# Unread products in TensorE's planned gaps, five early weight tiles, and the block mask as rows of the second score product

## Chip, core and metric

The kernel runs on one core of one Trainium2 chip. The metric is the device time of one execution in microseconds (us). The kernel before was timed at 738.15 us, the median of three runs from 735.75 to 738.77 us.

## What is computed

Three blocks follow one another on 4 sequences of 576 tokens. All inputs are float32.

```python
# attention: 8 heads of 64, causal by blocks of 64 tokens
scores = where(q_block >= k_block, q @ k.T / 8, -1e9)
x = softmax(scores) @ v                      # heads side by side: 512 features
# first mixture block, x_prev is x one token earlier
xk = mu_k * x + (1 - mu_k) * x_prev
xr = mu_r * x + (1 - mu_r) * x_prev
x = sigmoid(xr @ w_r) * (relu(xk @ w_k) ** 2 @ w_v)
# second mixture block
h = gelu_tanh(x @ w_in); u, v = halves(h)
out = x + (u * (w_sg @ layernorm(v) + b_sg)) @ w_out
```

## The kernel before

**Precision.** A float32 product is made of single-pass products in float32r: each operand is split into a high part and the rest, and three products are summed (high by high, high by rest, rest by high). The weights come as float64 words; `w_split` turns one tile of 128 x 512 of them into such a pair with two passes on ScalarE, four on VectorE and one on GpSimd. There are 20 such tiles for the first mixture block: 8 of `w_k`, 4 of `w_r`, 8 of `w_v`.

**Attention units.** A unit is one head of one sequence with either its first 320 tokens (`LO`, block rows 0 to 2) or its last 256 (`HI`, block rows 3 and 4); there are 64. The first 16 (`n < DIRECT`) are the `LO` units of sequences 0 and 1: their scores are plain float32 products, and two extra rows of the operands (66 rows in all) carry the block mask. For the other 48 units q and k lie twice, on partitions 0 to 63 and 64 to 127. `split_qk` makes `Q` (high part above, rest below), `K` (high part in both halves) and `KL` (the rest of k in both halves); `emit_S` then adds `Q` by `K` and `Q` by `KL` in PSUM, and between the two, for each block row but the first, a third product of 64 columns from `mask_l` and `mask_r`, which puts -2**33 on the last 64 columns for the first 64 queries of the row. That is two mask products a unit, 96 in all. Then come the maximum (VectorE), the exponential (ScalarE), the norm (VectorE), the transposes (`emit_T`) and the product with v (`emit_PV`), which writes the PSUM tile `O`; ScalarE copies `O` out to `xT`.

**Order.** Python code first lists all operations in an order of preference (`Order`, `attention`, `moe1`). `Plan.schedule` then simulates the engines with fixed costs (`takes`, `cost`) and lists every operation at its planned time, taking on each engine the ready operation that stands first in the list. That order is emitted; each engine works through its part of it strictly in order, and waits on the chip where the plan was too early. All loads go through SyncE's queue (SP). A weight load is planned behind the load that was listed before it (`op.behind`). The operations of all lines are emitted by one statement, so in the profile they all stand under L460, and the tile names tell them apart.

**First phase.** The eight `LO` heads of sequence 0 run first while the weights arrive; the heads' raw tiles share the ring `qkv` of three buffers (the first four heads use borrowed tiles). Then `moe1` works through eight halves of 288 tokens, with the attention units of the other sequences interleaved. Each half has the products with `w_k`, then `w_r`, then `w_v`. PSUM pool `ps1` serves all this and is closed at the start of the second mixture block.

The loads before the first attention step are issued by

```python
for n in range(5):
    load_head(n)
take(loads, 1)
```

and after that each second piece of attention work takes one more weight load.

Of the kernel before, what the change touches and what calls it, by code (L numbers as in the profile page):

```python
# [27 lines left out]

SHARE = dict(Kh=0.5, Qs=0.25, psc=0.25, xls=0.25)
calls = {}


# [39 lines left out]

class View:
# [195 lines left out]
    return d - 45, d, fn != "memset"  # L275


class Engine:
    def __init__(self, plan, name):
        self.plan, self.name = plan, name  # L280
# [5 lines left out]
class Plan:  # L286
# [2 lines left out]


    def __init__(self, tc):
        self.tc, self.nc, self.ops, self.last_dma = tc, tc.nc, [], None
        for e in ENG:
            setattr(self, e, Engine(self, e))

# [30 lines left out]
    def gate(self, closes, opens):  # L326
# [2 lines left out]
        self.ops.append(op)  # L329
        return op  # L330

    def schedule(self):
        for op in self.ops:
            if op.alts[0][0] == "gate":
                for p in op.alts[0][1]:
                    for o in p.ops:
                        op.preds[o.n] = o
        for op in self.ops:
            op.preds.pop(op.n, None)
            op.left = len(op.preds)  # L340
            for p in op.preds.values():
                p.succs.append(op)
        soon = {e: [] for e in ("PE", "ACT", "DVE", "POOL", "SP", "NONE")}
        ripe = {e: [] for e in soon}
        free = {e: 0.0 for e in soon}
        lock = dict(DVE=0.0, POOL=0.0)
        dma = 0.0
        order = []

        def offer(op):  # L350
            for x in op.tiles:
                if x.since is None:
                    x.waiters.append(op)
                    if len(x.waiters) == 1:
                        pump(x.ring)
                    return
            for i, a in enumerate(op.alts):
                e = ENG.get(a[0], "NONE")
                t = op.ready
                if op.preds:  # L360
                    t = max((p.run[0] if e == p.bi == "PE" or p is op.behind else p.end + LAT[e]) for p in op.preds.values())
                t = max([t] + [x.since + LAT[e] for x in op.tiles])
                heapq.heappush(soon[e], (t, op.n, i))

        def pump(ring):
            for x in ring.grant():
                for op in x.waiters:
                    offer(op)

        for r in {x.ring for op in self.ops for x in op.tiles}:  # L370
            r.tiles = [x for x in r.tiles if x.ops]
            for x in r.tiles:
                x.todo = len(x.ops)
        for op in self.ops:
            if not op.left:
                offer(op)
        while True:
            best = None
            for e in soon:
                for h in (ripe[e], soon[e]):  # L380
                    while h and self.ops[h[0][1] if h is soon[e] else h[0][0]].done:
                        heapq.heappop(h)
                if ripe[e]:
                    t = free[e]
                elif soon[e]:
                    t = max(free[e], soon[e][0][0])
                else:
                    continue
                if best is None or t < best[0]:
                    best = t, e  # L390
            if best is None:
                break
            t, e = best
            while soon[e] and soon[e][0][0] <= t:
                _, n, i = heapq.heappop(soon[e])
                heapq.heappush(ripe[e], (n, i))
            while self.ops[ripe[e][0][0]].done:
                heapq.heappop(ripe[e])
                if not ripe[e]:
                    break  # L400
            if not ripe[e]:
                continue
            n, i = heapq.heappop(ripe[e])
            op = self.ops[n]
            op.done, op.bi = True, e
            order.append((op, i))
            if e == "NONE":
                op.run, op.end = (t, t), t
            elif op.alts[i][1] == "dma_start":
                a = op.alts[i][2]  # L410
                v = next(x for x in a.values() if isinstance(x, View))
                rows = v.shape[0]
                size = v.cols * rows * 4 if not v.tile.dram else v.cols * 4
                if e == "SP":
                    free[e] = t + 375
                dma = max(t + 1400, dma) + size / (250.0 if rows != 66 else 172.0)
                op.run, op.end = (t, t + 375), dma + 150
            else:
                busy, d, port = takes(e, *op.alts[i][1:])
                s = t  # L420
                if port:
                    o = "POOL" if e == "DVE" else "DVE"
                    s = max(t, lock[o])
                end = max(s + d, t + d)
                free[e] = max(s + busy, end - (d - busy))
                if port:
                    lock[e] = end - (150 if e == "DVE" else 0)
                op.run, op.end = (s, free[e]), end
            for x in op.tiles:
                x.end = max(x.end, op.end)  # L430
                x.todo -= 1
                if not x.todo:
                    x.ring.slots.append(x.end)
                    pump(x.ring)
            for q in op.succs:
                q.left -= 1
                if not q.left:
                    offer(q)
        if len(order) < len(self.ops):
            o = next(o for o in self.ops if not o.done)  # L440
            seen = []
            while o not in seen:
                seen.append(o)
                o = next((p for p in o.preds.values() if not p.done), None) or next(
                    p for x in o.tiles if x.since is None for y in x.ring.tiles for p in y.ops if not p.done and p is not o)
            raise ValueError([(o.n, o.alts[0][:2], [(k, x.tile.args["tag"]) for k, x in o.alts[0][2].items() if isinstance(x, View)]) for o in seen[seen.index(o):]])
        self.order = order
        return max(o.end for o in self.ops)
# [49 lines left out]
def cost(n):  # L498
    return n / 2.4 + 13
# [3 lines left out]
def fused_kernel(ctx: ExitStack, tc: tile.TileContext, first, qkv_lo, qkv_hi, mu,  # L503
# [18 lines left out]
    def ptile(tag, cols, bufs):  # L522

        r = ring.setdefault(tag, [])
        if len(r) >= bufs:
            order.need(("ps", tag, len(r) - bufs))
        key = ("ps", tag, len(r))
        r.append(key)
        return ps([128, cols], F32, tag, bufs), key


    att_over = []
# [31 lines left out]
    nc.gpsimd.affine_select(out=ident, in_=ident, pattern=[[-1, 128]], compare_op=ALU.is_equal,  # L564
                            fill=0.0, base=0, channel_multiplier=1)

    mask_l = const([128, 128], F32R, "mask_l")
    mask_r = const([128, 64], F32R, "mask_r")
    nc.gpsimd.memset(mask_l.bitcast(F32), 0.0)
    nc.gpsimd.memset(mask_l[0:1, 0:64].bitcast(F32), 1.0)  # L570
    nc.gpsimd.memset(mask_r.bitcast(F32), -2.0 ** 33)
    mu_t = const([128, 2, 4], F32, "mu_t")
    um_t = const([128, 2, 4], F32, "um_t")
    x2d = [dram([4, 128, S], F32, f"x2d{b}") for b in range(B)]

    pcm, ps = pool("ps1", space=PSUM)
    mcm, mtile = pool("moe1")
    acm, atile = pool("attn", side="right")

# [11 lines left out]
    for t in pbuf:  # L591
        nc.gpsimd.memset(t[64:128, 0:64], 0.0)


    w1 = {}

# [62 lines left out]
    def split_qk(n):  # L659
# [4 lines left out]
        nq, nk = q.shape[1], k.shape[1]  # L664
        Q = atile([128, 320], F32R, "Q", 2)[:, 0:nq]
        K = atile([128, S], F32R, "K", 2)[:, 0:nk]
        KL = atile([128, S], F32R, "KL", 2)[:, 0:nk]
        copy(nc.scalar, Q, q)
        copy(act("Kh") if units[n][2] == HI else nc.scalar, K, k)
        sub(dve("Qs"), Q[64:128, :], q[64:128, :], Q[64:128, :].bitcast(F32))  # L670
        sub(nc.gpsimd, KL, k, K.bitcast(F32))
        splits[n] = (Q, K, KL)

    def split_v(n):
# [10 lines left out]

    def score_ns(n):
        f, cs = (2, CHUNKS[units[n][2]]) if n >= DIRECT else (4, CHUNKS[LO])
        return sum(f * cost(e - a) for c in cs for a, e in PIECES[c]) + cost(64) * (f == 2) * sum(c > 0 for c in cs)

    def out_ns(n, trans=True):  # L690
        kind = units[n][2]
# [3 lines left out]
    def emit_S(n):  # L695
# [18 lines left out]
        for c in chunks:  # L714
            q0, m, e, st = CH0[c] - TOKENS[kind][0], CHN[c], CHE[c], stc[c]
            for k0, k1 in PIECES[c]:
# [2 lines left out]
                    mm(o, Q[:, q0:q0 + m], K[:, k0:k1], start=True, stop=True)  # L719
                    continue  # L720
                mm(o, Q[:, q0:q0 + m], K[:, k0:k1], start=True)
                if c > 0 and k1 == e:
                    mm(st[:, e - 64:e], mask_l, mask_r)
                mm(o, Q[:, q0:q0 + m], KL[:, k0:k1], stop=True)

        def red(cs):
            for c in cs:
# [178 lines left out]
    def moe1():  # L906
# [3 lines left out]
        for i, (b, f) in enumerate(halves):  # L910
# [3 lines left out]
            for m in range(8):  # L914
# [18 lines left out]
                    nc.scalar.activation(out=R, in_=p, func=AF.Relu)  # L933

                def e1(R=R):
                    nc.scalar.activation(out=R, in_=R, func=AF.Square)

                def e2(R=R, m=m, kh=kh, kl=kl):
                    copy(nc.scalar, kh[:, m, :], R)
# [21 lines left out]
            for m in range(4):  # L961
# [3 lines left out]
                for g in range(0, 8, G):  # L965
# [2 lines left out]
                    pe(3 * G * cost(HF))  # L968
                    spent += 3 * G * cost(HF)
                    passes(p, "wv", 8, m, kh, kl, g, g + G)  # L970
                x2 = mtile([128, HF], F32, "x2", 2)

                def e4(p=p, m=m, x2=x2, th=th, b=b, f=f):
                    nc.vector.scalar_tensor_tensor(out=x2, in0=th[:, m, :], scalar=1.0, in1=p,
# [39 lines left out]
    early = [t[:, i] for tag in ("kh", "kl") for t in [mtile([128, 2, 960], F32, tag, 1)] for i in range(2)]  # L1014
    for n in range(5):
        load_head(n)
    take(loads, 1)
    nc.vector.tensor_scalar(out=um_t, in0=mu_t, scalar1=-1.0, scalar2=1.0, op0=ALU.mult, op1=ALU.add)
    split_qk(0)
    k = 0  # L1020
# [73 lines left out]
                pair(0, t, f * HF, (f + 1) * HF)  # L1094
    take(conv2, 99)
    order.run()
    pcm, ps = pool("ps2", space=PSUM, after=[pcm])
    ring.clear()

# [264 lines left out]
```

## Time and profile before

| | |
|---|---|
| median of 3 runs | 738.15 us |
| profiled execution | 739.07 us |
| its span, first to last instruction | 737.3 us |
| mean granted TensorE clock | 0.972 |
| busy share: matmul, weight load, VectorE, ScalarE, GpSimd | 95, 89, 72, 61, 41% |

PE is TensorE's matmul stream and PEld its weight loads; DVE is VectorE, ACT is ScalarE, POOL is GpSimd, SP is SyncE's queue. The shares are means over the whole span; the first 140 us differ from the rest. A granted clock of 1.00 is 2.4 GHz and 0.50 is 1.2 GHz. The 1.00 that the views give for the first stretch is a default and not a reading: two records of the product SB<-kh of 66 x 320 take 1.27 us at 5.01 us, and those of SB<-qkv of the same shape 0.70 us at 19.33 us. A float32 product stands in the trace as two matmul records, and some records are missing.

### The profile page before, as it was taken

The numbers are of one execution on the slowest core, as the hardware profiler recorded it, in microseconds if no ns is written. First come the engines' busy times: TensorE is split into PE (matmuls) and PEld (weight loads), VectorE is DVE, ScalarE is ACT, GpSimd is POOL, SyncE is SP. The second block draws the span as 40 slices with busy tenths as digits, with TensorE's granted clock in tenths as the row PEclk, the third lists the DMA queues.
The fourth block names the chain that finished last, engine by engine and source line by source line (L and its number), as shares of the span: only waits on it lengthen the run. The fifth ranks groups of instructions, "written<-read, shape, count | busy, mean of one in ns | idle before, by whom it ended". The sixth has DMA issues, their size and how long they took to land. (4 is left out here: it accounts for less than half of the span.)

```text
span 737.3 us, 13563 instructions
## 1 busy us (share of the span) xinstructions
PE 696.8 (95%) x4824; PEld 656.8 (89%) x4824; DVE 534.2 (72%) x1306; ACT 451.8 (61%) x1279; POOL 300.3 (41%) x349
## 2 busy tenths in 40 slices
PE   7859877899999999999999999999999999999998
PEld 5648665899999999999999999998898998998998
DVE  4888868788888777787888789679699546546323
ACT  3868755799689689799799689666353022022020
POOL 1235436576466346456567447132025012013021
PEclk9978886999999999999999999999999999999999
DMA  6196111522222222223231321072640120210101
GB/s 171 53 332 210 36 33 33 186 73 97 82 91 70 85 64 71 87 86 96 90 107 65 113 81 33 12 243 72 235 165 1 64 66 1 67 63 1 65 1 65
DMA packets 30722, 65.77 MB, mean 89 GB/s; under 512 B 5280, under 2 KB 16544, under 8 KB 30656
## 3 DMA queue, kind: packets, MB, share of 16 engines
q1 hardware_dynamic: 30512, 64.91, 27.4%
q8 instruction: 38, 0.62, 0.4%
q14 instruction: 28, 0.23, 0.1%
q10 hardware_dynamic: 144, 0.00, 0.0%
HBM read 55.47 MB, written 9.44 MB: 88 GB/s over the span
## 5 line engine op out<-in xcount | busy, mean ns | idle before, releaser
L460 PE MATMUL M<-xh,w 128*128 128x288 f32 x704 | 173.7, 313 | 5.9 <-ACT xh L460 2.5
L460 PEld LDWEIGHTS M<-xh,w 128*128 128x128 f32 x704 | 123.9, 194 | 9.0 <-ACT xh L460 2.8
L460 PE MATMUL M<-kh,w 128*128 128x288 f32 x432 | 106.3, 313 | 2.5 <-ACT w L460 1.3
L460 PE MATMUL M<-xl,w 128*128 128x288 f32 x352 | 107.1, 305 | 0.0
L460 PE MATMUL T<-ident,P 128*128 128x128 f32 x480 | 80.6, 286 | 12.8 <-DVE P L460 9.0
L460 DVE TENSOR_SCALAR_CACHE_REDUCE P<-P,rr 64x64 f32<-64x64 f32 (+3 forms) x160 | 79.6, 537 | 1.5
L460 POOL TENSOR_TENSOR KL<-qkv,K 128x576 fp32r<-128x576 f32 (+1 forms) x48 | 61.5, 1282 | 44.3 <-ACT K L460 35.3
L460 PEld LDWEIGHTS M<-kh,w 128*128 128x128 f32 x432 | 75.1, 192 | 4.5 <-ACT w L460 1.9
L460 ACT ACTIVATE PH<-T 128x384 fp32r<-128x384 f32 (+4 forms) x144 | 67.3, 478 | 19.1 <-PE T L460 17.9
L460 PEld LDWEIGHTS T<-ident,P 128*128 128x128 f32 x480 | 59.5, 145 | 20.9 <-DVE PL L460 8.7
L460 DVE TENSOR_TENSOR PL<-T,PH 128x256 fp32r<-128x256 f32 (+3 forms) x128 | 67.5, 543 | 13.6 <-ACT PH L460 12.6
L460 POOL TENSOR_TENSOR kl<-R,kh 128x288 fp32r<-128x288 f32 x64 | 56.1, 878 | 41.5 <-ACT kh L460 36.5
L460 PEld LDWEIGHTS M<-xl,w 128*128 128x128 f32 x352 | 68.7, 195 | 0.5 <-DVE u L460 0.2
L460 POOL TENSOR_TENSOR gt<-gt,U 128x288 f32<-128x288 f32 x32 | 28.2, 884 | 99.7 <-DVE gt L460 97.6
L460 POOL TENSOR_TENSOR w<-u,w 128x512 fp32r<-128x512 f32 x24 | 36.4, 1516 | 75.7 <-ACT w L460 65.9
L460 PE MATMUL M<-kl,w 128*128 128x288 f32 x216 | 65.4, 303 | 0.0
L460 POOL TENSOR_TENSOR xl<-t,xh 128x288 fp32r<-128x288 f32 x48 | 40.5, 843 | 58.9 <-ACT xh L460 53.8
L460 ACT ACTIVATE U<-M 128x288 f32<-128x288 f32 x32 | 13.0, 410 | 71.7 <-PE M L460 71.7
L460 PE MATMUL O<-gh,w 128*128 128x288 f32 x256 | 52.4, 297 | 1.0 <-DVE o L460 1.0
L460 DVE SCALAR_TENSOR_TENSOR u<-w,u 128x512 int32<-128x512 int32 x64 | 51.9, 817 | 0.2
L460 PE MATMUL M<-XHL,w 128*128 128x288 f32 x384 | 51.9, 295 | 0.0
L460 PE MATMUL O<-PH,V 128*128 128x256 f32 (+2 forms) x208 | 51.5, 278 | 0.1
(182 smaller groups left out, 1935.1 us busy)
## 6 DMA issues: line engine op xcount, KB each, us to landing
qkv<-qkv_hi_dram SPq DMA_DIRECT2D x32, 576.0 KB, 3.6
qkv<-qkv_lo_dram SPq DMA_DIRECT2D x16, 416.0 KB, 3.4
x2d<-x SPq DMA_DIRECT2D x32, 144.0 KB, 1.8
X<-x2d SPq DMA_DIRECT2D x4, 1152.0 KB, 12.3
outT_dram<-o SPq DMA_DIRECT2D x32, 144.0 KB, 1.8
w<-w_k_dram SPq DMA_DIRECT2D x8, 512.0 KB, 11.1
w<-w_v_dram SPq DMA_DIRECT2D x8, 512.0 KB, 9.5
w<-w_in_dram SPq DMA_DIRECT2D x8, 512.0 KB, 8.6
```

The lines of the kernel that those rows point to most:

```text
L460: getattr(getattr(self.nc, e), fn)(*pos, **{k: real(x) for k, x in a.items() if k[0] != "_"})
```

## The change

The fillers: `plan.fill` names one product, 64 x 192 from a tile `calm` of zeros, written to the last 192 columns of the PSUM tile `O`, which nobody reads. Where the plan has TensorE idle for over 300 ns before an operation, from planned time 1500 ns on and until `ps1` is closed, `schedule` puts copies of it ahead of that operation, for 70% of the gap. `O` becomes one fixed tile (`one_o`) in place of a ring of one. The planner now also keeps a model of the clock (`Gate`), by which a product is planned at twice its time while the clock is low, and a limit of eight transfers under way.

The loads: five weight tiles are listed before the first attention step in place of one.

The mask: `q2` and `k2` hold on partitions 64 to 127 the mask's rows, written once at the start on GpSimd (`mask_rows`, ten operations of 576 columns on a `qkv` buffer and the four tiles). For each of the 48 units `k2` gets the rest of k on partitions 0 to 63, and `q2` gets the high part of `Q` there by a transfer from SBUF to SBUF on SP's queue. The second score product takes these two; the mask products are gone, and so is the product of the two rests.

Further: the output tile `x2` is now `th` in place, and `SHARE` has an entry `r2` that nothing uses.

```diff
+FILL = 192
+FILL_DUTY = 0.7
+GATE_AT = -2000.0
...
+class Gate:
...
+    def fill(self, at, e, fn, **a):
+        self.filler, self.filler_from = Op(-1), at
+        self.filler.alts = ((e, fn, a),)
...
             if e == "NONE":
                 op.run, op.end = (t, t), t
+                if self.filler and self.filler.alts[0][2]["out"].tile.pool in op.alts[0][1]:
+                    self.filler = None
...
+                t = max(t, lanes.pop(0) + 40)
...
+                lanes.append(op.end)
             else:
                 busy, d, port = takes(e, *op.alts[i][1:])
                 s = t
+                if e == "PE":
+                    gap = t - free[e]
+                    if self.filler and self.filler_from <= t and gap > 300:
+                        x = gate.step(free[e])
+                        f = cost(FILL) * x
+                        k = int((gap - 100 - max(0, self.filler_from - free[e])) * FILL_DUTY / f)
+                        at = max(free[e], self.filler_from)
+                        for _ in range(k):
+                            order.insert(len(order) - 1, (self.filler, 0))
+                            gate.add(at, at + FILL / 2.4 * x)
+                            at += f
+                    x = gate.step(t)
+                    gate.add(t, t + min(busy, busy - 10) * x)
+                    d += busy * (x - 1)
+                    busy *= x
...
-        return ps([128, cols], F32, tag, bufs), key
+        return one_o if tag == "O" and one_o else ps([128, cols], F32, tag, bufs), key
...
+    calm = const([128, FILL], F32R, "calm")
+    nc.gpsimd.memset(calm.bitcast(F32), 0.0)
...
+    one_o = ps([128, 512], F32, "O")
+    plan.fill(1500.0, "tensor", "matmul", out=one_o[0:64, 512 - FILL:512], lhsT=calm[:, 0:64], rhs=calm, start=True, stop=True)
...
+    q2 = [atile([128, S], F32R, f"q2{i}") for i in range(2)]
+    k2 = [atile([128, S], F32R, f"k2{i}") for i in range(2)]
+    def mask_rows():
+        t = atile([128, 1152], F32, "qkv", 3)
+        for o, value, first, rows in ((0, -2.0 ** 33, 128, k2), (S, 1.0, 64, q2)):
+            a = t[:, o:o + S]
+            nc.gpsimd.memset(a, value)
+            for sign, base in ((1, -first), (-1, first + 63)):
+                nc.gpsimd.affine_select(out=a, in_=a, pattern=[[sign, S]], compare_op=ALU.is_ge, fill=0.0,
+                                        base=base + sign * 64 * 128, channel_multiplier=-sign * 128)
+            for r in rows:
+                nc.gpsimd.tensor_copy(out=r[64:128, :], in_=a[64:128, :])
...
-        KL = atile([128, S], F32R, "KL", 2)[:, 0:nk]
+        KL = k2[n % 2][:, 0:nk]
+        t0, t1 = TOKENS[units[n][2]]
         copy(nc.scalar, Q, q)
+        nc.sync.dma_start(out=q2[n % 2][0:64, t0:t1].bitcast(F32), in_=Q[0:64, :].bitcast(F32))
...
-        sub(nc.gpsimd, KL, k, K.bitcast(F32))
+        sub(nc.gpsimd, KL[0:64, :], k[0:64, :], K[0:64, :].bitcast(F32))
...
-                if c > 0 and k1 == e:
-                    mm(st[:, e - 64:e], mask_l, mask_r)
-                mm(o, Q[:, q0:q0 + m], KL[:, k0:k1], stop=True)
+                mm(o, q2[n % 2][:, CH0[c]:CH0[c] + m], KL[:, k0:k1], stop=True)
...
-                x2 = mtile([128, HF], F32, "x2", 2)
+                x2 = th[:, m, :]
...
-    take(loads, 1)
+    take(loads, 5)
+    mask_rows()
```

## Rows read from the trace of the kernel before

**Rows 1.** The page, part 2: granted TensorE clock in 40 slices, tenths.

```profile
PEclk9978886999999999999999999999999999999999
```

**Rows 2.** Windows: length, busy us (instructions) by engine, granted clock, DMA share, GB/s.

```profile
0.00:18.25 18.25, 13.80 (x40) 9.63 (x41) 7.73 (x37) 7.05 (x26) 1.85 (x22) 1.00 0.62 173
18.25:45.55 27.30, 20.80 (x112) 15.40 (x110) 21.24 (x68) 20.83 (x66) 6.59 (x6) 1.00 0.44 144
45.55:62.62 17.07, 13.39 (x43) 10.57 (x44) 13.89 (x26) 10.34 (x24) 7.89 (x7) 0.50 1.04 337
...
83.10:127.47 44.37, 35.68 (x152) 28.82 (x151) 34.07 (x85) 25.07 (x69) 20.23 (x14) 0.73 0.11 35
...
200.00:300.00 100.00, 97.90 (x761) 96.02 (x760) 78.37 (x214) 87.33 (x269) 56.15 (x74) 1.00 0.24 75
```

**Rows 3.** Windows: sum over the five stretches at clock 0.50 between 83 and 127.5.

```profile
sum 23.87, PE 21.90 PEld 17.93 DVE 21.91 ACT 9.34 POOL 14.10; mean PE 4.38 PEld 3.59 DVE 4.38 ACT 1.87 POOL 2.82
```

**Rows 4.** Waits of PE, 0 to 140 us: total us, times, longest.

```profile
PE T L460 <- DVE P L460: 9.0, 7, 2.5
PE SA L460 <- ACT P L460: 5.1, 5, 1.6
```

**Rows 5.** Waits of PE, 140 to 470 us, the largest.

```profile
PE T L460 <- DVE PL L460: 2.9, 10, 0.5
```

**Rows 6.** Timeline of PE in a HI unit's scores: start, us, instruction.

```profile
465.11 0.36 PE L460 MATMUL SA<-K,Q 128*128 128x448 f32 x1
...
465.63 0.29 PE L460 MATMUL SB<-K,Q 128*128 128x288 f32 x1
...
465.89 0.30 PE L460 MATMUL SB<-K,Q 128*128 128x288 f32 x1
...
466.27 0.30 PE L460 MATMUL M<-xh,w 128*128 128x288 f32 x1
```

**Rows 7.** Instructions on tile mask_l: ns min/median/max, first and last start.

```profile
L460 PE MATMUL SA<-mask_r,mask_l x48: 191/193/278, 130.2 to 465.3; 128*128 128x64 f32 x48
```

**Rows 8.** Lines by shape, 0 to 140 us: VectorE passes of weight splitting, busy, mean ns.

```profile
L460 DVE SCALAR_TENSOR_TENSOR u<-w,u 128x512 int32<-128x512 int32 x40 | 35.3, 883 | 0.1
...
L460 DVE TENSOR_SCALAR u<-u 128x512 int32<-128x512 int32 x20 | 12.0, 600 | 0.1
...
L460 DVE TENSOR_SCALAR u<-u 128x512 f32<-128x512 f32 x20 | 10.7, 540 | 9.7 <-ACT u L460 9.5
```

**Rows 9.** Timeline of SP's queue, 0 to 40 us.

```profile
5.21 0.43 SPq L460 DMA_DIRECT2D w<-w_k_dram  x1
...
9.01 0.34 SPq L460 DMA_DIRECT2D qkv<-qkv_lo_dram  x1
31.66 0.31 SPq L460 DMA_DIRECT2D qkv<-first_dram  x1
...
32.40 4.01 SPq L460 DMA_DIRECT2D w<-w_k_dram  x6
```

**Rows 10.** Timeline of PE: first score product of head 5.

```profile
21.81 0.85 PE L460 MATMUL M<-qkv 66*64 66x64 f32 x4
```

**Rows 11.** Timeline of ACT and of PE: one unit's Q copy, its second product.

```profile
304.82 0.46 ACT L460 ACTIVATE Q<-qkv 128x320 fp32r<-128x320 f32 x1
...
316.21 0.22 PE L460 MATMUL SA<-KL,Q 128*64 128x64 f32 x1
```

**Rows 12.** The page, part 6: transfers, KB each, median us to landing.

```profile
x2d<-x SPq DMA_DIRECT2D x32, 144.0 KB, 1.8
```

**Rows 13.** Waits of SP's queue, whole span, the largest.

```profile
SPq L460 <- POOL V L460: 247.4, 45, 9.1
```

**Rows 14.** Timeline of POOL, 0 to 40 us.

```profile
1.17 0.29 POOL L460 TENSOR_SCALAR_AFFINE_SELECT ident<-ident 128x128 f32<-128x128 f32 x1
...
24.09 1.27 POOL L460 TENSOR_TENSOR w<-u,w 128x512 fp32r<-128x512 f32 x1 [21.37 <-ACT w L460]
```

**Rows 15.** Instructions on tile O, 40 to 130 us: ns min/median/max, first and last start.

```profile
L460 ACT ACTIVATE xT<-O x9: 430/432/433, 41.5 to 128.5; 64x320 f32<-64x320 f32 x9
```

More of the change, by code (lines that the diff above doesn't have):

```diff
@@ L27 @@
 F64_MAX = struct.unpack("f", struct.pack("I", (1151 << 20) - 1))[0]
-SHARE = dict(Kh=0.5, Qs=0.25, psc=0.25, xls=0.25)
+SHARE = dict(Kh=0.5, Qs=0.25, psc=0.25, r2=0.5, xls=0.25)
 calls = {}
@@ L275, in takes, with __init__, step, add @@
     return d - 45, d, fn != "memset"
+class Gate:
+    WINDOW = 4096 / 1.2
+    def __init__(self, at):
+        self.edge, self.used, self.slow = at, {}, True
+    def step(self, t):
+        while self.edge + self.WINDOW <= t:
+            u = self.used.pop(round(self.edge), 0.0) / self.WINDOW
+            self.slow = u < (0.88 if self.slow else 0.47)
+            self.edge += self.WINDOW
+        return 2.0 if self.slow else 1.0
+    def add(self, a, b):
+        e = self.edge
+        while e < b:
+            n = min(b, e + self.WINDOW) - max(a, e)
+            if n > 0:
+                self.used[round(e)] = self.used.get(round(e), 0.0) + n
+            e += self.WINDOW
 class Engine:
@@ L291, in __init__ @@
     def __init__(self, tc):
-        self.tc, self.nc, self.ops, self.last_dma = tc, tc.nc, [], None
+        self.tc, self.nc, self.ops, self.last_dma, self.filler, self.filler_from = tc, tc.nc, [], None, None, 0.0
         for e in ENG:
@@ L346, in schedule @@
         lock = dict(DVE=0.0, POOL=0.0)
-        dma = 0.0
+        dma, lanes = 0.0, [-40.0] * 8
         order = []
+        gate = Gate(GATE_AT)
         def offer(op):
@@ L565, in fused_kernel @@
                             fill=0.0, base=0, channel_multiplier=1)
[L567 to L571, printed above, removed]
+    calm = const([128, FILL], F32R, "calm")
+    nc.gpsimd.memset(calm.bitcast(F32), 0.0)
     mu_t = const([128, 2, 4], F32, "mu_t")
@@ L687, in score_ns @@
         f, cs = (2, CHUNKS[units[n][2]]) if n >= DIRECT else (4, CHUNKS[LO])
-        return sum(f * cost(e - a) for c in cs for a, e in PIECES[c]) + cost(64) * (f == 2) * sum(c > 0 for c in cs)
+        return sum(f * cost(e - a) for c in cs for a, e in PIECES[c])
     def out_ns(n, trans=True):
@@ L935, in e1 @@
                 def e1(R=R):
-                    nc.scalar.activation(out=R, in_=R, func=AF.Square)
+                    if True:
+                        nc.scalar.activation(out=R, in_=R, func=AF.Square)
+                    else:
+                        nc.gpsimd.tensor_tensor(out=R, in0=R, in1=R, op=ALU.mult)
                 def e2(R=R, m=m, kh=kh, kl=kl):
@@ L1096, in fused_kernel @@
     order.run()
+    one_o = None
     pcm, ps = pool("ps2", space=PSUM, after=[pcm])
```

## The prediction

> **What bounds the kernel now.** I read the clock strip of the page first [rows 1]: the clock is down in stretches before slice 8 and full after it, so the kernel has two parts with different limits. The windows say which [rows 2]. From 200 to 300 us TensorE's matmuls are busy 97.9 of 100 us at full clock, VectorE 78.4 and ScalarE 87.3: TensorE sets the pace, and its largest wait between 140 and 470 us is 2.9 us in ten pieces [rows 5]. What is taken from TensorE's queue there comes straight off the end.
>
> Before 140 us it is different. From 45.55 to 62.62 the clock is at 0.50, its 1.2 GHz level, TensorE is busy only 13.4 of 17.1 us, and VectorE 13.9; from 83.1 to 127.5 it is 35.7 and 34.1 of 44.4, at a mean clock of 0.73 [rows 2]. Looking only at the five stretches at 0.50 in there [rows 3], VectorE is busy 21.9 of 23.9 us, which is more telling than TensorE's 21.9, because TensorE's share is stretched by the low clock and VectorE's is not. So in the dips TensorE waits on VectorE, and the low clock follows the waiting: its longest waits in the phase are for VectorE's normalised P (9.0 us, up to 2.5 at a time) and for ScalarE's exponentials (5.1 us) [rows 4]. VectorE is loaded by the weight splits: 35.3 + 12.0 + 10.7 = 58.0 us for 20 tiles, 2.9 us a tile [rows 8]. And these come late because of SP's queue: it issues its last early transfer at 9.01, then stands still until 31.66 behind a head's load that needs a free buffer, and only then come six more tiles of `w_k` [rows 9].
>
> **The change part by part.** I sum against the profiled execution's 739.07 us (span 737.3 and 1.8 around it); the median of the runs stands 0.9 below it.
>
> *Mask products, 96 removed.* The timeline gives the price by start to start [rows 6]. Two plain products of 288 columns take 465.89 - 465.63 = 0.26 us; the next two with a mask product between them take 466.27 - 465.89 = 0.38. The mask costs 0.12. The other one: 465.63 - 465.11 = 0.52 for two of 448 columns and a mask; 448 columns by the 288 rate are 0.13 x 448/288 = 0.20 (an estimate from those rows), leaving again 0.12. So 96 x 0.12 = 11.5 us. Bounds: if only the 64 columns counted, 0.13 x 64/288 = 0.03 each, 2.8 us, but the two spacings exclude that; if the whole recorded 0.191 [rows 7] were free, 18.3, which they exclude too. They are rounded to 0.01, so I keep 10.5 to 12.5. Nearly all lie between 130.2 and 465.3 us [rows 7], in the TensorE-bound part. I take 11.5 off.
>
> *The transfer of Q into q2, 48 added.* It takes the place of nothing on TensorE, but the second product now waits for it. One unit's Q copy ends at 304.82 + 0.46 = 305.28 and its second product starts at 316.21 [rows 11], two units later: 10.9 us of cover. The nearest transfer is the one of 144 KB for x2d, 1.8 us to landing [rows 12]. Ahead of it in SP's queue may stand a load that waits for a buffer: 247.4 us in 45 waits, 5.5 on average, 9.1 at most [rows 13]. 5.5 + 1.8 = 7.3 is covered; 9.1 + 1.8 = 10.9 just so. I take 0. Without the cover, 48 waits of some 2 us would be 96 us, so this term is safe only while the copies run two units ahead. Behind a waiting Q transfer stand the next head's load and x2d; the loads themselves wait 5.5 us on average for a buffer, which leaves room.
>
> *Four more weight tiles early.* Before, SP got two tiles out ahead of the standstill; with five listed ahead it gets at least five. VectorE could use them in its idle time: from 18.25 to 45.55 it is busy 21.24 of 27.30 [rows 2], so 6.06 us are idle, room for two tiles of 2.9. What is done there is missing later, when VectorE sets the pace. Not all idle pieces will fit, and the attention's own VectorE work comes between: I take 4 off, with bounds 0 and 6. The price: the five transfers stand on SP's queue ahead of the loads of head 5, whose first product is at 21.81 [rows 10]. Five tiles of 0.52 MB at the 173 GB/s of the first window [rows 2] take 15 us from 5.2 on, until 20.4. That is still covered, by 1.4 us. I take 0, bound 3.
>
> *Unread products.* A product of 192 columns at full clock is about 0.13 x 192/288 = 0.09 us (an estimate from rows 6). Where the chip has the gap that the plan has, it costs nothing. What it may return is the clock. TensorE is busy 13.4 us in the long low stretch and 21.9 in the five short ones, 35.3 us; at twice the clock 17.6 us are saved at most, if nothing else held TensorE. But VectorE is busy 92% of the five and 81% of the long one, so most of that turns into waiting. What comes back is the idle share of VectorE in these stretches, 2.0 + 3.2 = 5.2 us; I take 4, bounds 0 and 17.6. The first 18 us I leave as they are: matmuls are busy 13.8 us of 18.25 there, after a start at 3.8, so there are few gaps to fill.
>
> One rule of the Trainium skill speaks against this part. In this case's rows `O` is copied out by ScalarE in 0.43 us, nine times between 40 and 130 us [rows 15], and no row shows a product written beside a copy in the same tile. The page "PSUM — Partial Sum Buffer", section "PSUM bank collisions raise a hardware error", says that TensorE's writes and another engine's reads must be kept apart by whole bank and group of 32 partitions, even where the columns differ. The fillers share that bank with `O`, so by this rule each batch behind a product with v would wait for the copy. If no such batch found its wait covered, 9 x 0.43 = 3.9 us would be added, and the sum would be 3.9 us higher; this is a rival below.
>
> *mask_rows.* Ten GpSimd passes of 576 columns. The nearest row is a select of 128 columns, 0.29 us [rows 14]; by columns 1.3 each, 13 us in all as a ceiling. GpSimd is idle for 21.4 us before its first real work at 24.09 [rows 14], so I take 0. `x2` in `th`, `r2`: same instructions, 0.
>
> *Sum.* 739.07 - 11.5 - 4 - 4 = 719.6 in a profiled execution, 718.7 in the median: I say 719.
>
> **Rivals.** (A) *VectorE takes the first phase's gain back.* The clock rises, but the wait for P stays. For it: VectorE's 92% in the dips. Against: its 6 idle us before 45. Only the mask counts: 739.1 - 11.5 = 727.6, median 727.
>
> (B) *The unread products do not hold the clock.* The change doesn't do that part; the dips stay. For it: the phase's low clock also holds while TensorE is busy by its own account. Mask and loads count, some products are in the way: 739.1 - 11.5 - 4 + 1.5 = 725, median 724.
>
> (C) *Each batch waits for the copy of O*, the mechanism priced above: 718.7 + 3.9 = 723. The copies are prompt, which speaks against much of it.
>
> (D) *The phase comes loose altogether.* Splits fit all of VectorE's early idle time and the clock never falls: 739.1 - 11.5 - 6 - 17.6 = 704, median 703. For it: 14 us of waits on P and the exponentials, which shorten when TensorE's part of that chain is faster. Against: VectorE's total.
>
> (E) *Slower: the plan's gaps are not the chip's gaps.* The products are put in by the plan's clock, and TensorE works strictly in order, so each one without a real gap adds its 0.09 us. To undo the 19.5 us of gain takes 19.5/0.09 = 217 of them, some 28 us of planned gap (70% filled) that the chip doesn't have; from 258 on, 23.2 us, the kernel is slower by over 0.5%. Between 140 and 470 us the chip hardly waits [rows 5], so if the plan has 10% of gaps there, that decides it. With 320 such products: 719 + 28.8 = 748.
>
> **How the numbers follow.** Forecast, 712 to 726: 0.38. A 0.17, B 0.10, C 0.08, D 0.14, E 0.13, of which 0.08 end slower and 0.05 within 0.5% (3.7 us, about what a measurement here can tell from no change). Faster is forecast, A, B, C and D: 0.87. The range runs from D's 704 to 733, where A ends if the mask gives its least (10.5) and 4 to 5 us of products are uncovered; it leaves out half of D and E, 0.2.
>
> **What the profile after would show.** Mask: no `mask_l` rows, and start to start between score products 0.13 throughout; TensorE still over 97% busy from 200 to 300 us. Transfer: no wait of TensorE for a q2 transfer. Loads: five transfers of `w_k` before 10 us, and GpSimd's first split well before 24 us. Clock: no stretch at 0.50 after 18 us, and products from `calm` in the first 140 us only. The prediction is wrong if `calm` products stand between 140 and 470 us in number (E), if VectorE's share before 128 us rises without the end of the phase moving (A), or if that stretch gains over 15 us (D).

## The result, and the profile after

The changed kernel takes 713.26 us in the median of four runs (712.72 to 714.59), against 738.46 for the kernel before on the same chip: ratio 0.9666, 95% interval 0.9635 to 0.9697, some 25 us less. The profiled execution is 713.72 us with a span of 712.0. The forecast was 719 with a range of 704 to 733. The direction and the range held; the time is 5.7 us below the forecast. Executions of the kernel before differ in granted clock: of 13 on another chip, the six at 0.981 took 734.8 to 735.8 us and the seven at 0.972 to 0.977 took 736.3 to 739.6, so differences of 1 or 2 us need the intervals below.

The clock strip of the page, which answers to [rows 1]:

```profile
PEclk9999999999999999999999999999999999999999
```

The windows of [rows 2] again, in the changed kernel (length, busy us and instructions of PE, PEld, DVE, ACT, POOL, clock, DMA share, GB/s):

```profile
0.00:18.25 18.25, 14.49 (x42) 9.73 (x43) 8.46 (x37) 7.18 (x26) 7.85 (x30) 1.00 0.86 271
18.25:45.55 27.30, 22.86 (x161) 18.50 (x159) 25.32 (x71) 19.40 (x59) 9.02 (x7) 1.00 0.27 80
45.55:62.62 17.07, 15.48 (x114) 13.46 (x115) 14.35 (x30) 12.86 (x35) 7.94 (x7) 1.00 1.02 346
...
83.10:127.47 44.37, 41.23 (x284) 35.80 (x283) 39.42 (x107) 33.05 (x99) 25.89 (x20) 1.00 0.32 95
200.00:300.00 100.00, 98.84 (x770) 97.19 (x768) 75.37 (x234) 87.25 (x278) 54.98 (x72) 1.00 0.31 90
```

The clock no longer falls: 1.00 where it was 0.50 and 0.73. TensorE's busy share is no measure of progress here, since it holds the unread products; VectorE's is. It does 25.3 us of work from 18.25 to 45.55 (21.2 before) and 39.4 from 83.1 to 127.5 (34.1 before). From 200 to 300 us nothing but the mask products is gone from TensorE's queue, and it still sets the pace.

Where the time went shows in the first and last start of the split units' score products, to be held against [rows 7] (tile `q2` is printed as q; the second row are the transfers into it):

```profile
L514 PE MATMUL SA<-k,q x64: 218/320/450, 116.2 to 441.9; 128*128 128x448 f32 x32, 128*64 128x64 f32 x16, 128*128 128x192 f32 x16
L514 SPq DMA_DIRECT2D q<-Q x48: 467/467/1418, 108.8 to 430.5; - x48
```

The first start moved from 130.2 to 116.2, so the first phase gave 14.0 us where the prediction added up 8, just short of the 15 by which rival D was to be told. The last moved from 465.3 to 441.9: the stretch between them, where 94 of the 96 mask products stood, gave 9.4 more. The end moved by 25.3 in the span, so a further 1.9 came after the last scores, which nothing in the prediction accounts for.

The timeline of one unit's scores, against [rows 6]:

```profile
441.72 0.36 PE L514 MATMUL SA<-K,Q 128*128 128x448 f32 x1
441.92 0.37 PE L514 MATMUL SA<-k,q 128*128 128x448 f32 x1
442.13 0.29 PE L514 MATMUL SB<-K,Q 128*128 128x288 f32 x1
442.26 0.29 PE L514 MATMUL SB<-k,q 128*128 128x288 f32 x1
442.39 0.29 PE L514 MATMUL SB<-K,Q 128*128 128x288 f32 x1
```

Two products of 448 columns take 442.13 - 441.72 = 0.41 us where they and a mask product took 0.52; two of 288 still take 0.26, where with a mask they took 0.38.

The unread products (tile `calm`), and TensorE's largest waits from 0 to 140 us, against [rows 4]:

```profile
L514 PE MATMUL O<-calm x204: 247/252/496, 1.2 to 117.9; 128*64 128x192 f32 x102
```

```profile
PE O L514 <- ACT xT L514: 5.3, 6, 1.7
PE SA L514 <- DMA kh<-first_dram: 1.8, 1, 1.8
PE O L514 <- POOL calm L514: 1.2, 1, 1.2
PE SA L514 <- ACT P L514: 0.9, 2, 0.6
PE SA L514 <- DMA q<-Q: 0.7, 1, 0.7
```

All 204 stand before 118 us. The waits for P (9.0 us) and for the exponentials (5.1, now 0.9) have given way to them, and the largest wait is new: unread products that wait for ScalarE's copy out of `O`.

SP's queue, against [rows 9]:

```profile
5.18 3.85 SPq L514 DMA_DIRECT2D w<-w_k_dram  x5
...
10.36 0.43 SPq L514 DMA_DIRECT2D w<-w_k_dram  x1
...
37.30 0.31 SPq L514 DMA_DIRECT2D qkv<-first_dram  x1
```

Six tiles go out before the standstill in place of two; the standstill itself is still there and ends later, at 37.30. GpSimd's first part of a weight split, which the prediction wanted well before 24 us, starts only 1.6 us earlier than in [rows 14]:

```profile
22.48 1.28 POOL L514 TENSOR_TENSOR w<-u,w 128x512 fp32r<-128x512 f32 x1 [13.64 <-ACT w L514]
```

### The profile page after: what moved, and what is told of

Same layout as the page of the kernel before. It is cut to its first block, busy times and chain, and to the rows that moved or that the text cites. A ratio compares the mean times of both kernels' runs of the same rounds, so it can differ in the third digit from the quotient of the medians.

```text
span 712.0 us, 13974 instructions
## 1 busy us (share of the span) xinstructions
PE 688.5 (97%) x4932; PEld 652.0 (92%) x4932; DVE 525.6 (74%) x1306; ACT 449.6 (63%) x1279; POOL 306.2 (43%) x357
## 4 chain that ended last, share of the span: by engine, by line
PE 63%; ACT 18%; DVE 9%; issue 3%; POOL 3%; DMA 3%; SPq 1%; POOLq 0%; ACTq 0%; DVEq 0%
PE M L514 32%; PE O L514 13%; PE T L514 6%; PE V L514 5%; ACT P L514 5%; PE SA L514 3%; ACT R L514 3%; PE SB L514 2%; DVE P L514 2%; DVE PL L514 2%; ACT PH L514 1%; ACT kh L514 1%; DMA w<-w_v_dram 1%; ACT otmp L514 1%; ACT t L514 1%
## 5 line engine op out<-in xcount | busy, mean ns | idle before, releaser
L514 PE MATMUL M<-xh,w 128*128 128x288 f32 x704 | 167.8, 305 | 1.1 <-ACT R L514 0.8
L514 PEld LDWEIGHTS M<-xh,w 128*128 128x128 f32 x704 | 120.0, 188 | 2.7 <-ACT R L514 1.7
L514 PE MATMUL M<-kh,w 128*128 128x288 f32 x432 | 104.4, 307 | 0.6 <-POOL w L514 0.5
L514 PE MATMUL M<-xl,w 128*128 128x288 f32 x352 | 104.5, 298 | 0.3 <-POOL xl L514 0.3
L514 PE MATMUL T<-ident,P 128*128 128x128 f32 x480 | 76.5, 277 | 5.2 <-DVE PL L514 4.1
L514 POOL TENSOR_TENSOR k<-qkv,K 64x576 fp32r<-64x576 f32 (+1 forms) x48 | 62.7, 1307 | 29.5 <-ACT K L514 18.7
L514 PEld LDWEIGHTS T<-ident,P 128*128 128x128 f32 x480 | 57.5, 141 | 12.2 <-DVE PL L514 9.4
L514 PEld LDWEIGHTS M<-xl,w 128*128 128x128 f32 x352 | 66.3, 188 | 0.7 <-POOL xl L514 0.5
L514 DVE SCALAR_TENSOR_TENSOR u<-w,u 128x512 int32<-128x512 int32 x64 | 54.5, 855 | 0.3
L514 PE MATMUL O<-PL,V 128*128 128x256 f32 (+2 forms) x208 | 51.4, 285 | 0.7 <-DVE PL L514 0.6
```

Of the source, the lines that this page charges most:

```text
L514: getattr(getattr(self.nc, e), fn)(*pos, **{k: real(x) for k, x in a.items() if k[0] != "_"})
```

## The experiments

Twelve kernels besides the change, each against the kernel before on its own chip. What a ratio lacks to 1, or the difference of two ratios, times 738 us gives the microseconds quoted; behind a difference stands its 95% half width, from the two intervals added in squares. In e4 to e6 and e9 to e13 the planner also puts no unread product between the products of an open sum in the tile that they share; this was not tried by itself, but e9, which has it beside its own edit, is level with the change.

| kernel | median us | ratio | 95% interval |
|---|---|---|---|
| the change | 713.26 | 0.9666 | 0.9635 to 0.9697 |
| e1_mask_only | 726.31 | 0.9873 | 0.9829 to 0.9917 |
| e2_loads_only | 735.45 | 0.9992 | 0.9975 to 1.0009 |
| e3_not_emitted | 719.84 | 0.9763 | 0.9728 to 0.9799 |
| e4_fill_only | 727.29 | 0.9870 | 0.9843 to 0.9896 |
| e5_loads1 | 717.95 | 0.9739 | 0.9714 to 0.9764 |
| e6_other_bank | 719.47 | 0.9762 | 0.9715 to 0.9808 |
| e8_x2_in_place | 736.65 | one run | |
| e9_full_clock_plan | 713.55 | 0.9670 | 0.9653 to 0.9686 |
| e10_plan_only | 722.98 | 0.9806 | 0.9764 to 0.9849 |
| e11_duty035 | 717.01 | 0.9720 | 0.9694 to 0.9747 |
| e12_duty100 | 716.91 | 0.9722 | 0.9700 to 0.9745 |
| e13_loads8 | 710.69 | 0.9640 | 0.9618 to 0.9662 |

**e1_mask_only**: the kernel before with the mask part of the diff (and `x2` in `th`).

```diff
-                if c > 0 and k1 == e:
-                    mm(st[:, e - 64:e], mask_l, mask_r)
-                mm(o, Q[:, q0:q0 + m], KL[:, k0:k1], stop=True)
+                mm(o, q2[n % 2][:, CH0[c]:CH0[c] + m], KL[:, k0:k1], stop=True)
```

> The kernel before with the mask rows alone (second product from q2 and k2, Q transfer, mask_rows); no unread products, one early weight tile. Theory that the mask is worth its 96 products: 738.5 - 11.5 = 727, the first scores of a split unit still at about 130 us, and the stretch from there to the last unit's scores shorter by 10 to 12 us. Rival, that the transfers of Q cost what the products gave: 735 or more, with waits of TensorE for them.

It gave 1.27%, 9.4 us, with 3.2 either way; `x2` in `th` is a part of this. Its second products start at 128.5 and 453.6:

```profile
L460 PE MATMUL SA<-k,q x64: 219/320/474, 128.5 to 453.6; 128*128 128x448 f32 x32, 128*64 128x64 f32 x16, 128*128 128x192 f32 x16
```

Between them lie 325.1 us, 10.0 less than the 335.1 of [rows 7]; the start moved by 1.7. The first theory holds, and the transfers of Q cost nothing that can be seen.

**e2_loads_only**: the kernel before with five early tiles.

```diff
-    take(loads, 1)
+    take(loads, 5)
```

> The kernel before with five weight tiles listed early in place of one, nothing else. Theory of the prediction (VectorE's idle time takes two tiles): 734, with the low clock's stretches still there. Rival, that early splits only push the attention's work back while VectorE sets the pace: 738 or more. Rival, that the loads are the main thing in the first phase: 728 or less.

0.08% less, 0.6 us, not distinguishable from none. Alone the early tiles do not pay the 4 us of the prediction. In the clock strip the dips are not gone but moved:

```profile
PEclk9767998999999999999999999999999999999999
```

The low stretch now begins in the second slice, some 18 us earlier than before. The clock is low for 44.4 us here against 40.9 before, and VectorE is idle for 12.8 of them against 5.1 (its sum over the low stretches, against [rows 3] and the long one in [rows 2]):

```profile
sum 44.40, PE 38.20 PEld 30.00 DVE 31.56 ACT 26.24 POOL 15.62; mean PE 9.55 PEld 7.50 DVE 7.89 ACT 6.56 POOL 3.91
```

This fits early splits that leave TensorE waiting earlier; the cause of that shift was not tried by itself.

**e3_not_emitted**: the changed kernel with its own plan, and the unread products left out when the program is written.

```diff
         for op, i in self.order:
+            if op.n == -1:
+                continue
             e, fn, a = op.alts[i]
```

> The changed kernel with the same plan and order, but the unread products are left out of the program. If they hold the clock and the clock makes the first phase short: the clock falls again between 20 and 130 us and the time is 721 to 727 (8 to 14 us lost against 713.3). Rival, that the new order and the early tiles make the gain: 711 to 716, whatever the clock does.

719.84, ratio 0.9763 against 0.9666: the unread products are worth 0.97%, 7.2 us (3.5 either way), with everything else in the same order. The clock falls again without them, as these windows show:

```profile
18.25:45.55 27.30, 18.68 (x78) 13.93 (x77) 24.93 (x71) 18.98 (x58) 8.95 (x7) 0.80 0.25 74
45.55:62.62 17.07, 11.68 (x54) 9.11 (x53) 13.43 (x27) 11.06 (x29) 6.42 (x5) 0.80 1.03 358
```

It ends 1.2 us short of the range expected, and the rival that order and tiles make all of the gain falls. The clock is low in five stretches, 34.2 us in all, in which VectorE is busy for 28.5:

```profile
sum 34.20, PE 30.12 PEld 24.30 DVE 28.51 ACT 17.35 POOL 15.32; mean PE 6.02 PEld 4.86 DVE 5.70 ACT 3.47 POOL 3.06
```

**e6_other_bank**: the changed kernel with the unread products in the last 192 columns of the score tile `SB` (1024 columns), where the first phase's scores take columns 0 to 319.

```diff
-    one_o = ps([128, 512], F32, "O")
+    one_o = ps([128, 1024], F32, "SB")
...
-out=one_o[0:64, 512 - FILL:512]
+out=one_o[0:64, 1024 - FILL:1024]
```

> The changed kernel with the unread products written to the second half of the score tile SB, which the first phase does not use, in place of O (and none between the products of an open sum). If their waits for the copy of O (5.3 us in six waits) stand in the way of real work: 708 to 711, and no wait of an unread product for ScalarE's copy. Rival, that what follows them waits anyway: 712 to 714.

Neither: 719.47, slower than the change. Its largest waits of TensorE from 0 to 140 us, and two of the places:

```profile
PE SB L517 <- ACT P L517: 5.5, 3, 2.2
PE SB L517 <- DVE stats L517: 3.3, 4, 1.4
```

```profile
27.02 2.08 PE L517 MATMUL SB<-calm 128*64 128x192 f32 x21 [1.25 <-ACT P L517]
...
39.24 1.99 PE L517 MATMUL SB<-calm 128*64 128x192 f32 x20 [1.36 <-DVE stats L517]
```

The products now wait for the readers of the scores, in columns that they don't touch: in this program the wait goes by the tile. Right behind two such waits, of 2.1 and 2.2 us, the clock falls:

```profile
109.00:116.00 7.00, 7.00 (x33) 6.29 (x32) 5.25 (x13) 2.09 (x5) 6.84 (x6) 0.51 0.04 9
122.80:129.60 6.80, 5.84 (x27) 5.37 (x26) 3.67 (x14) 4.53 (x13) 3.99 (x5) 0.50 0.11 33
```

That is a part of the loss only, since two of the four executions show a mean clock of 1.00 and still took 715.7 and 717.7 us. What the wait for the copy of `O` costs the changed kernel is not settled; a tile without other readers was not tried.

**e4_fill_only** and **e5_loads1**: the changed kernel with one early tile, and e4 with the old mask products as well (`x2` stays in `th`).

```diff
-    take(loads, 5)
+    take(loads, 1)
```

> The changed kernel with the old mask products and one early weight tile: unread products and the planner's clock model alone (no batch between the products of an open sum). If the unread products and the new plan are worth 8 us or so by themselves: 727 to 731 against 736 to 738 for the kernel before, clock held from about 18 us on. Rival, that they pay only together with the early tiles, since TensorE waits for weights otherwise: 734 or more.

> The changed kernel with one early weight tile in place of five (no batch between the products of an open sum). If the early tiles are worth what they were alone (0.8 us, e2_loads_only): 713 to 715. Rival, that with the clock held they remove waits for weights: 717 to 721, with waits of TensorE for split weights between 40 and 60 us.

e4: 0.9870, 9.6 us, from unread products, the new plan and `x2` in place; the rival falls. The two kernels differ in the mask alone, which is worth 1.31% here, 9.7 us (2.7 either way), with the clock held in both. e5: 0.9739 against 0.9666, so the early tiles are worth 0.73%, 5.4 us (2.9 either way), once the clock is held. That is the rival's number, but the waits for split weights that it expected are small here:

```profile
PE M L517 <- POOL w L517: 0.5, 1, 0.5
PE M L517 <- ACT w L517: 0.4, 1, 0.4
```

With one tile the gaps before the weights are filled with unread products, which hide the waits; the next run takes them out.

**e10_plan_only**: e5_loads1 with the unread products left out, by the edit of e3.

> The kernel of e5_loads1 (the change with one early weight tile), same plan and order, with the unread products left out of the program. If the unread products are worth the same with and without the early tiles: some 7 us above e5_loads1, a ratio of 0.983 to 0.986, which is also that of e1_mask_only, so the new planner is worth nothing by itself. Rival, that the planner's new order is worth some us by itself: 0.976 to 0.980. Rival, that early tiles and unread products only work together: 0.974.

0.9806. TensorE's waits for split weights from 0 to 140 us are now in the open:

```profile
PE M L519 <- ACT w L519: 6.2, 5, 1.9
PE M L519 <- POOL w L519: 3.2, 4, 1.3
```

With five tiles, in e3_not_emitted, the same two rows add up to 0.8 us. So the early tiles do remove waits for split weights, as the rival of e5 has it, though only 1.5 of the 9.4 us lie between 40 and 60 us, where it looked for them. The unread products are worth 0.67% (4.9 us, 3.6 either way) with one early tile and 0.97% with five; the early tiles 0.43% (3.2 us, 4.1 either way, so not clear of none) without them and 0.73% with them. Whether the two help each other is not shown by these four numbers. Whether the new planner is worth anything by itself stays open: e10 is 4.9 us below e1_mask_only, and their intervals overlap.

**e9_full_clock_plan**: a planner that takes the clock as full.

```diff
-        return 2.0 if self.slow else 1.0
+        return 1.0
```

> The changed kernel with a planner that takes the clock as full throughout (no batch between the products of an open sum); unread products still in the planned gaps. If the planner's model of the low clock matters for the order in the first phase: 716 to 720. If it does not: 712 to 715.

0.9670 with 196 unread products: beside them the planner's model of the low clock shows no gain.

**e11_duty035** and **e12_duty100**: how much of the gaps is filled.

```diff
-FILL_DUTY = 0.7
+FILL_DUTY = 0.35   # e12: 1.0, and gap > 150 for gap > 300
```

> The changed kernel with the planned gaps filled to 35% in place of 70% (76 unread products in place of 204; none between the products of an open sum). If the clock falls again for want of work: stretches at 0.50 between 20 and 130 us and 716 to 720. If it holds with fewer: 711 to 714, and then some of the 204 had been in the way.

> The changed kernel with gaps from 150 ns on filled to 100% (305 unread products; none between the products of an open sum). If uncovered products delay real work: 101 more at 0.09 us, up to 9 us, 714 to 722. If the chip has the gaps: 712 to 714, the clock held as in the changed kernel; if more work also raises the clock before 16 us: below 711.

Both lose 4 us against the change (3 either way). With 76 products the clock falls again:

```profile
PEclk9887999999999999999999999999999999999999
```

With 305 it is held, and the 101 more cost 0.56%, 4.1 us, 0.04 each: about half of them lie in real gaps, if each uncovered one costs 0.09.

**e8_x2_in_place**: one edit, to explain the 1.9 us after the last scores.

```diff
-                x2 = mtile([128, HF], F32, "x2", 2)
+                x2 = th[:, m, :]
```

> The kernel before with x2 written in place into th, nothing else. All kernels with the change's mask part lost a wait of 1.7 us of TensorE near 503 us (tile SA, for VectorE's x2). If x2 in place is the reason: that wait is gone and the stretch from the last unit's scores to the first product of the second block takes 54.2 us in place of 56.3. If not: 56.3 and the wait is there.

The largest wait of TensorE after the last scores, in the kernel before, then the only one here:

```profile
PE SA L460 <- DVE x L460: 1.7, 1, 1.7
```

```profile
PE T L460 <- DVE PL L460: 0.2, 1, 0.2
```

The wait is gone, and from the start of the last unit's scores (464.4) to the end of the span (734.8) it takes 270.4 us, against 272.2 (465.1 to 737.3) before. The change takes 270.3, from 441.7 to 712.0. The term is `x2` in place. VectorE has no idle time before the operation that TensorE waited for, so it came late by the order: it starts at 503.3 in the kernel before, and in place at 487.7.

**e13_loads8**: eight early tiles.

```diff
-    take(loads, 5)
+    take(loads, 8)
```

> The changed kernel with eight early weight tiles in place of five (none of the unread products between the products of an open sum). If VectorE has no idle time left in the first 45 us (25.3 of 27.3 us busy with five): 713 to 717, since heads 5 to 7 come later. If more early tiles still help: 708 to 711.

710.69, the lowest median of the study: 0.9640 against 0.9666, 1.9 us, with 2.8 either way, so not clear of the change; the rival of 713 to 717 falls. The first split scores start at 114.4:

```profile
L517 PE MATMUL SA<-k,q x64: 218/322/472, 114.4 to 438.3; 128*128 128x448 f32 x32, 128*64 128x64 f32 x16, 128*128 128x192 f32 x16
```

## Why the prediction was right, step by step

*Mask products: right, size a little high.* The spacings give 0.11 and 0.12 us each, against the 0.12 predicted, which would be 94 x 0.115 = 10.8 in the stretch; 9.4 arrived there, 10.0 in e1, and the times of e4 and e5 are 9.7 apart. TensorE's waits show part of the rest; from 118 to 450 us the changed kernel has

```profile
PE T L514 <- DVE PL L514: 4.1, 11, 1.1
PE M L514 <- ACT R L514: 0.8, 2, 0.5
```

and four small ones, 6.9 us in all, where 5.0 stood before between 140 and 470. That a shorter TensorE queue meets VectorE and ScalarE more often fits this; it was not tried by itself.

*Transfers of Q: right.* The prediction took 1.8 us from x2d's transfers; these land in 2.0 us (1.9 to 3.6). The cover held: TensorE waited for one of the 48, 0.7 us for the second unit at 121.7 us. The prediction's sign of no such wait failed by that one.

*Early tiles: the size by luck.* 4 us were predicted as a term of its own. Alone they give 0.6, without unread products under the new plan 3.2, and with them 5.4, so that the 4 lies among numbers of which only the last is clear of none. The mechanism, VectorE's idle time from 18.25 to 45.55, is there: it fell from 6.06 to 1.98 us, 4.1 us of work. But the same idle time fell to 3.8 us in e2_loads_only and gave nothing at the end.

*Unread products: right in kind, too small.* This is the term of the sum that was mis-sized: 4 predicted, 7.2 measured (e3_not_emitted, 3.5 either way) and 4.9 with one early tile (e10). "What comes back is the idle share of VectorE in these stretches" was the reasoning, with 5.2 us for the kernel before, of which 4 were taken. In e3_not_emitted, the changed kernel without them, the low stretches lie elsewhere and hold 5.7 us of idle VectorE (34.20 - 28.51), which is within the error of what was measured. From 0 to 128 us VectorE's busy time, of the kernel before, e3_not_emitted and the change, is

```profile
0.00:128.00 128.00, 101.89 (x459) 80.42 (x460) 96.83 (x263) 81.56 (x241) 49.05 (x61) 0.84 0.40 125
```

```profile
0.00:128.00 128.00, 102.15 (x486) 81.71 (x487) 98.84 (x277) 86.50 (x260) 58.43 (x72) 0.87 0.42 136
```

```profile
0.00:128.00 128.00, 115.07 (x739) 96.56 (x740) 104.85 (x292) 92.25 (x276) 63.52 (x77) 1.00 0.47 148
```

31.2 us idle before, 29.2 with the new order and tiles at a falling clock, 23.2 with the clock held: from e3 to the change 6.0 us of VectorE's idle time went, about as much as it had in the low stretches. This bears the reasoning out, by the rows of another order than the one it was taken from; whether idle time between the low stretches came back too is not shown. That the unread products hold the clock (rival B fails) is shown by the strip and by e3 and e11 together, and rival A fails because the end of the phase moved.

*The new plan: no term at all.* The prediction took nothing for the planner's new order. It may be worth 4.9 us (e10 against e1), which is not clear of noise; this stays open.

*The wait for the copy of O: happened, price open.* Unread products waited 5.3 us in six waits for the copy. This agrees with the rule of the Trainium skill that the prediction weighed ("PSUM — Partial Sum Buffer", section "PSUM bank collisions raise a hardware error"), in that the program keeps the two apart. The trace doesn't test that rule: in e6 the waits go by the tile, whatever the columns. That the change is faster than the 723 of rival C doesn't settle the price either, since other terms came out larger than predicted.

*mask_rows: right*, about 6 us of GpSimd done by 8.5 us. *x2 in place: wrong*; "same instructions, 0" overlooked that with buffers of its own the output is planned later, while TensorE waits for the PSUM tile that this operation reads. It gave 1.9 us.

*Rival E did not come, but e12 fits its mechanism:* there the 101 products more cost time, 0.04 us each on average against the 0.09 that E gave to each uncovered one. In the change none stands after 118 us.

One path from the kernel before to the change, each step the difference of two ratios: mask and `x2` 9.4 us (e1), the new plan 4.9 (e10, not clear of noise), unread products 4.9 (e5) and early tiles 5.4 (the change). Their sum is the 24.6 of the change by construction and is no test; by way of e3 the early tiles are 3.2 and the unread products 7.2. By the starts in the two profiles the gain of the span splits into 14.0 us up to the first split scores (8 predicted), 9.4 from there to the last (11.5) and 1.9 behind them (0). The last two errors cancel by luck; the first phase is what made the forecast too small.

## What to carry to other kernels

Price a removed product by start to start in the stream around it, not by its columns: 64 columns cost 0.115 us here beside 0.13 for 288. Where TensorE takes turns with another engine, estimate the gain of a held clock from the other engine's idle time in the low stretches, and take these from the order that the new kernel will have: here 5.2 us by the old order, 5.7 by the new, and 7.2 measured. Here unread products held the clock only when enough of the gaps was filled, and cost time when all were: 35% and 100% both lost 4 us against 70%. A product that fills a gap also hides a wait from the list of waits; the waits show again when the products are left out.

## What was not expected of the hardware

Products of zeros are enough to hold the clock: 204 of 64 x 192 kept it at 1.00 from 18 us on, and without them it fell to 0.50 five times. And the clock did not rise early in any run. In the change matmuls were busy for 14.5 of the first 18.25 us, yet two records of 66 x 320 took 1.27 us at 10.54 and 0.70 at 19.37. In e9, with 16 unread products before 13 us, matmuls were busy for 15.8 of them, and two such records still took 1.27 us at 14.87.
